# Activation biases as numbers, long runs for k, v and phi, and another order of the first loads

## The chip, the core and the metric

The kernel runs on one core of a Trainium2 chip. The metric is the device time of one execution in microseconds, as the median of several runs. In the profile PE is TensorE (PEld its weight loads), ACT is ScalarE, DVE is VectorE, POOL is GpSimd and SP is SyncE, which issues every DMA of this kernel.

## The reference

A memory attention (8 batches, 8 heads, 576 tokens, head size 64, 32 memory slots) followed by a feed-forward block with its own activation:

```python
a = softmax of phi over the tokens                  # b h s m
k_m = np.einsum('bhsm,bhsd->bhmd', a, k)
v_m = np.einsum('bhsm,bhsd->bhmd', a, v)
attn = softmax over m of (q @ k_m^T / sqrt(64))
x = (attn @ v_m) as 4608 tokens x 512
h = x @ w_in                                        # 512 x 2048, float64
sp = np.maximum(h, 0.0) + np.log1p(np.exp(-np.abs(h)))
out = ((h * erf(sp)) @ w_out)                       # 2048 x 512, float64
```

## The kernel before

The host lays the inputs out anew and hands the two weight matrices over as 64-bit integers. The chip turns these doubles into floats: `decode_1` clamps the high words on DVE (L142) and converts low and high words on ACT (L145, L146), `decode_2` joins them on DVE (L159, L162), and `decode_3` splits a w_out piece into a high and a low part (ACT L174 and L179, PE L177 and L178). A whole piece of weights has 1 MB and stands in a slot of the tag `wo`; smaller ones of half a MB stand in the three `raw` slots, which k and v use too.

A batch goes through `phi_max`, `phi_exp`, `kmvm` (k_m and v_m on PE, L275), `block_diag`, and `vw`, which multiplies v_m with w_in, so that the first matrix product of the feed-forward block takes the attention weights directly. The tokens of a batch are two units of 288. A unit has eight steps, one for each 256 columns of w_in: `ffn1` (PE L390, then tt = Tanh on ACT L397 and a product on DVE L398), three `factor`s (f on ACT L411 or L413, a product on DVE L414), `g_split` (ACT L422, DVE L423), and, up to three steps later, `ffn2` (PE L437), which sums into four PSUM tiles pso. After eight steps ACT L453 copies these out and SP stores them. The kernel has 128 steps.

The activation function is a product of the tt term and three factors with constants in a table. Each constant that is added ahead of the activation stands in a column of 128 x 1 in SBUF (`tb`, `fb`) and is given to the instruction as its bias:

```python
tb = column(GB, "tb")                                          # L104
nc.scalar.activation(tt[:, j], ps, AF.Tanh, bias=tb, scale=0.5)   # L397
```

k, v and phi are loaded so that chunk c of a tile holds tokens 128c to 128c + 127, one token to a partition, and the last chunk the remaining 64 tokens in 64 partitions. So a k/v tile of two heads comes in four DMAs (L210 and L214, for k and for v) with runs of 512 bytes, and phi in two (L193, L197) with runs of 1 KB.

The program is a list of tasks, written out ahead in the order of the steps, with the decoding and the next batch's tasks merged in. Loads have a queue of their own: each waits for a slot of its tag, and `FIRST` says in which order the first slots are given out. The final order on each engine is set by the framework's scheduler; on SP and on each engine instructions then issue in order. Batch 0's k/v tiles 0 and 1 must be there for the first `kmvm`, all four for the second, and w_in piece 0 for the first `vw`.

Of the kernel before, what the change touches and what calls it, by code (L numbers as in the profile page):

```python
# [8 lines left out]
F32 = mybir.dt.float32  # L9
# [4 lines left out]
AF = mybir.ActivationFunctionType  # L14
# [13 lines left out]
GC, GB = 0.27160413, -0.45239282  # L28
FACTORS = (
    ("Q", -1.75972316, 0.52065829),  # L30
    ("T", 0.56841178, 1.0199725, 0.42607248),
    ("T", 1.35008185, -1.89147316, 1.73987114),
)
# [3 lines left out]
def tile_memory_attention_then_erf_softplus_ffn(  # L37
    ctx: ExitStack,
    tc: tile.TileContext,
    qT: bass.AP,  # L40
    k: bass.AP,
    v: bass.AP,
    phi: bass.AP,
    phiT: bass.AP,
    w_in: bass.AP,
# [3 lines left out]
    nc = tc.nc  # L49
    P = 128  # L50
    B, _, S = qT.shape
    H = k.shape[2]
    D = 64
    M = 32
    DFF = w_in.shape[2]
# [1 line left out]
    NDM = DM // P  # L57
    NP_ = H // 2
    NG = 2
# [6 lines left out]
    SC = [(c * P, min(P, S - c * P)) for c in range((S + P - 1) // P)]  # L66
    RAW_BUFS = 3
    STAGED = 6
    FIRST = "wo phiT start phi wo raw raw wo raw start wo q".split()
    LEAD = 7  # L70
    WINDOW = {mybir.EngineType.DVE: (12, 28)}
    PO = 5
# [5 lines left out]
    const = ctx.enter_context(tc.tile_pool(name="const", bufs=1))  # L78
# [17 lines left out]
    ones = const.tile([P, P], F32, name="ones")  # L96
    nc.vector.memset(ones, 1.0)

    def column(value, name):
        t = const.tile([P, 1], F32, name=name)  # L100
        nc.vector.memset(t, value)
        return t

    tb = column(GB, "tb")  # L104
    fb = [column(f[1] if f[0] == "Q" else f[2], f"fb{i}") for i, f in enumerate(FACTORS)]
    fd = [f[2] if f[0] == "Q" else f[3] for f in FACTORS]

    w_in_sb = {}
    wo = {}
# [8 lines left out]
    st = {}  # L118
# [62 lines left out]
    def load_phiT(b, g):  # L181
# [4 lines left out]
        nc.sync.dma_start(out=t, in_=phiT[b, g * P : (g + 1) * P, :])  # L186
        st["phiT", b, g] = t

    def load_phi(b):
        t = att.tile([P, len(SC), H * M], F32, name="phi")  # L190
        n = S // P
        s0, ln = SC[-1]
        nc.sync.dma_start(  # L193
            out=t[:, :n], in_=phi[b, : n * P].rearrange("(c p) e -> p c e", p=P)
        )
        if ln < P:
            nc.sync.dma_start(out=t[:ln, n], in_=phi[b, s0 : s0 + ln])  # L197
        st["a", b] = t

    def load_kv(b, p):  # L200
        if b == 0 and p == NP_ - 1:
            t = wop.tile([P, len(SC), 2, 2, D], F32, name="kv", tag="wo")
        else:
            t = raw_pool.tile([P, len(SC), 2, 2, D], F32, name="raw")
        n = S // P
        s0, ln = SC[-1]
        h = 2 * p
        for x, src in enumerate((k, v)):
            src = src[b, :, h : h + 2]
            nc.sync.dma_start(  # L210
                out=t[:, :n, x], in_=src[: n * P].rearrange("(c p) h e -> p c h e", p=P)
            )
            if ln < P:
                nc.sync.dma_start(out=t[:ln, n, x], in_=src[s0 : s0 + ln])  # L214
        for j in range(2):
            st["kv", b, h + j] = t[:, :, :, j, :]

    def load_q(u):
        b, hf = divmod(u, 2)
# [19 lines left out]
    def phi_exp(b):  # L239
        ps = ps_a.tile([P, H * M], F32, name="psa")  # L240
        for g in range(NG):
            nc.tensor.matmul(
                out=ps[:, g * P : (g + 1) * P],
                lhsT=ones,
                rhs=st["diag", b][:, g],
                start=True,
                stop=True,
            )
        a = st["a", b]
        n = S // P  # L250
        ln = SC[-1][1]
        nc.vector.tensor_tensor(
            out=a[:, :n], in0=a[:, :n],
            in1=ps.unsqueeze(1).to_broadcast([P, n, H * M]), op=ALU.add,
        )
        if ln < P:
            nc.vector.tensor_tensor(out=a[:ln, n], in0=a[:ln, n], in1=ps[:ln], op=ALU.add)
            nc.scalar.activation(a[:ln, n], a[:ln, n], AF.Exp)
        nc.scalar.activation(a[:, :n], a[:, :n], AF.Exp)  # L259
        for g in range(NG):  # L260
            sm = st.pop(("psm", b, g))
            rs = small.tile([P, 1], F32, name=f"prs{g}")
            nc.vector.tensor_scalar_add(out=sm, in0=sm, scalar1=1e-9)
            nc.vector.reciprocal(out=rs, in_=sm)
            st["prs", b, g] = rs
# [108 lines left out]
    def products(w, x):  # L374
        return [(w[a], x[b]) for a, b in ((0, 0), (0, 1), (1, 0))]

    def ffn1(i, j):
        u, c = divmod(i, NPR)
        at, w = st["at", u], st["vw", u // 2, c]
        if j == 0:  # L380
            st["el", i] = (
                el.tile([P, 2, U], F32, name="tt"),
                el.tile([P, 2, U], F32, name="acc", bufs=3),
            )
        tt, acc = st["el", i]
        ps = ps_h.tile([P, U], F32, name="psh")
        parts = products(w, at)
        for k, (x, y) in enumerate(parts):
            for g in range(NG):
                nc.tensor.matmul(  # L390
                    out=ps,
                    lhsT=x[:, g, j * P : (j + 1) * P],
                    rhs=y[:, g, :],
                    start=(k + g == 0),
                    stop=(k == len(parts) - 1 and g == NG - 1),
                )
        nc.scalar.activation(tt[:, j], ps, AF.Tanh, bias=tb, scale=0.5)  # L397
        nc.vector.scalar_tensor_tensor(  # L398
            out=acc[:, j], in0=tt[:, j], scalar=1.0, in1=ps, op0=ALU.add, op1=ALU.mult
        )  # L400
        if j == 1 and u % 2 == 1:
            st.pop(("vw", u // 2, c))
        if j == 1 and c == NPR - 1:
            st.pop(("at", u))
# [72 lines left out]
    for c in range(NPR):  # L477
        n = NP_ if c < STAGED else 2
# [3 lines left out]
    def decode_steps(a, b):  # L482
        out = []
        for n in range(a, b):
            out.append((decode_1, *pieces[n]))
            for back, f in ((1, decode_2), (2, decode_3)):
                if n >= back:
                    out.append((f, *pieces[n - back]))
        if b == len(pieces):
            out += [(decode_2, *pieces[-1])] + [(decode_3, *p) for p in pieces[-2:]]  # L490
        return out
# [20 lines left out]
    for i in range(NPR):  # L512
        n = min(2 * i + 2 + LEAD, len(pieces))
# [5 lines left out]
    d = decode_steps(0, LEAD)  # L519
# [6 lines left out]
    for i in range(NS + 3):  # L526
        head = [(ffn1, i, 0)] if i < NS else []
        rest = []
        if 1 <= i <= NS:
            head += [(factor, i - 1, 1)]  # L530
        if i < NS:
            head += [(ffn1, i, 1)]
        if 1 <= i <= NS:
            rest += [(factor, i - 1, 2)]
        if i < NS:
            rest += [(factor, i, 0)]
        if 2 <= i <= NS + 1:
            rest += [(g_split, i - 2)]
        if i >= 3:
            rest = merge([(ffn2, i - 3, d) for d in range(NDM)], rest)  # L540
        prog += head + (merge(rest, side[i]) if i < NS else rest)

    def loads(f, a):
        if f is kmvm:
            kv = [("raw", load_kv, a[0], 2 * a[1] + r) for r in range(2)]
            if a == [0, NG - 1]:
                kv[1] = ("start", *kv[1][1:])
            return kv
        if f is decode_1:
            return [("wo" if a[3] == NP_ else "raw", load_weight, *a)]  # L550
        if f is phi_max:
            return [("start" if a == [0, 1] else "phiT", load_phiT, *a)]
        if f is phi_exp:
            return [("phi", load_phi, *a)]
        if f is scores:
            return [("q", load_q, a[0])]
        return []
# [28 lines left out]
    held, room = room, dict.fromkeys(room, 0)  # L586
    for tag in FIRST:
        room[tag] += 1
# [9 lines left out]
    for n, (f, *a) in enumerate(prog):  # L598
        start = len(traced)
        f(*a)  # L600
        for x in traced[start:]:
            if x.engine in issued:
                q, w = issued[x.engine], WINDOW[x.engine][n >= HEAD]
# [40 lines left out]
```

## Time and profile before

| | |
|---|---|
| median of 3 runs | 791.09 us (790.6 to 791.68) |
| the profiled execution | 790.4 us |
| its span, first to last instruction | 788.5 us |
| mean granted TensorE clock | 0.985 |
| DMA, whole span | 64.99 MB, 69514 packets, 82 GB/s |

The page gives the share of busy time of each engine over the whole span; the kernel has a beginning of about 100 us, in which the weights are decoded, and a long even part. A table by stretches of time and the chain of waits tell them apart. In the groups of instructions the number behind the busy time is the mean duration in ns; in the table of DMA issues the last number is the median time from issue to landing.

### The profile page before, as it was taken

How to read it: one execution, taken by the hardware profiler on the slowest of the kernel's cores; microseconds unless marked ns; L12 is line 12 of the kernel's file. 1: busy time of each engine (PE TensorE's matmuls, PEld its weight loads, DVE VectorE, ACT ScalarE, POOL GpSimd, SP SyncE). 2: the span in 40 equal slices, each digit the busy share in tenths (PEclk: the TensorE clock that was granted, in tenths of full speed). 3: DMA queues.
4: the chain of work that ended last, by engine and by line, in shares of the span. 5: the costliest groups of instructions: out<-in, count | busy, mean ns of one | idle time of the engine just before them, and what ended most of it. 6: DMA issues, size and time to landing. Idle time of an engine off the chain costs nothing.

```text
span 788.5 us, 15764 instructions
## 1 busy us (share of the span) xinstructions
PE 750.3 (95%) x6192; PEld 666.4 (85%) x6192; DVE 663.6 (84%) x1145; ACT 632.7 (80%) x1164; POOL 0.7 (0%) x6
## 2 busy tenths in 40 slices
PE   2668899999999999999999999999999999999998
PEld 1246678789988899888988899889988899889998
DVE  4699787889979897988979798989979897889874
ACT  4699778678887878878887878878888888788784
POOL 0000000000000000000000000000000000000000
PEclk9986999999999999999999999999999999999999
DMA  9983326303060203302060203302060201100000
GB/s 275 359 316 107 86 87 171 100 1 91 13 200 1 75 18 106 106 1 91 19 193 2 76 17 109 104 1 91 18 194 1 77 1 54 40 1 31 2 31 31
DMA packets 69514, 64.99 MB, mean 82 GB/s; under 512 B 4160, under 2 KB 62016, under 8 KB 68672
## 3 DMA queue, kind: packets, MB, share of 16 engines
q1 hardware_dynamic: 69440, 63.98, 26.2%
q8 instruction: 49, 0.80, 0.4%
q14 instruction: 25, 0.20, 0.1%
HBM read 54.53 MB, written 9.44 MB: 81 GB/s over the span
## 4 chain that ended last, share of the span: by engine, by line
PE 85%; ACT 7%; DMA 5%; DVE 2%; SPq 1%; issue 1%; ACTq 0%; DVEq 0%
PE pso L437 49%; PE psh L390 25%; PE psa L308 6%; PE psa L275 3%; DMA phiT<-phiT 1%; DMA w_in<-w_in 1%; DMA raw<-k 1%; PE psa L177 1%; DMA raw<-v 1%; DVE acc L414 1%; ACT f L413 1%; ACT tt L397 1%; ACT wo L179 1%; ACT w_in L145 1%; ACT w_out L146 1%
## 5 line engine op out<-in xcount | busy, mean ns | idle before, releaser
L437 PE MATMUL pso<-g_hi,wo 128*128 128x288 f32 x2048 | 436.3, 298 | 1.0 <-ACT g_hi L422 1.0
L437 PEld LDWEIGHTS pso<-g_hi,wo 128*128 128x128 f32 x2048 | 336.7, 189 | 26.5 <-issue 13.6
L414 DVE SCALAR_TENSOR_TENSOR acc<-f,acc 128x576 f32<-128x576 f32 x384 | 289.7, 754 | 34.7 <-ACT f L411 10.6
L437 PE MATMUL pso<-g_lo,wo 128*128 128x288 f32 x1024 | 302.3, 296 | 1.0 <-DVE g_lo L423 1.0
L437 PEld LDWEIGHTS pso<-g_lo,wo 128*128 128x128 f32 x1024 | 193.7, 189 | 2.6 <-DVE g_lo L423 1.3
L413 ACT ACTIVATE f<-tt,fb 128x576 f32<-128x576 f32 x256 | 185.1, 766 | 1.9 <-DVE acc L414 1.9
L397 ACT ACTIVATE tt<-psh,tb 128x288 f32<-128x288 f32 x256 | 121.9, 497 | 44.3 <-PE psh L390 43.0
L398 DVE SCALAR_TENSOR_TENSOR acc<-tt,psh 128x288 f32<-128x288 f32 x256 | 111.1, 449 | 23.6 <-ACT tt L397 22.9
L423 DVE SCALAR_TENSOR_TENSOR g_lo<-acc,g_hi 128x576 fp32r<-128x576 f32 x128 | 96.2, 751 | 28.7 <-ACT g_hi L422 25.9
L390 PE MATMUL psh<-at_hi,vw_hi 128*128 128x288 f32 x512 | 116.2, 308 | 4.3 <-ACT at_hi L115 2.6
L422 ACT ACTIVATE g_hi<-acc 128x576 fp32r<-128x576 f32 x128 | 87.3, 682 | 39.8 <-DVE acc L414 33.7
L390 PE MATMUL psh<-at_lo,vw_hi 128*128 128x288 f32 x512 | 110.9, 298 | 0.0
L390 PE MATMUL psh<-at_hi,vw_lo 128*128 128x288 f32 x512 | 109.8, 296 | 0.0
L390 PEld LDWEIGHTS psh<-at_hi,vw_hi 128*128 128x128 f32 x512 | 82.5, 191 | 23.3 <-DVE acc L414 10.1
L411 ACT ACTIVATE f<-tt,fb 128x576 f32<-128x576 f32 x128 | 99.5, 778 | 3.1
L390 PEld LDWEIGHTS psh<-at_hi,vw_lo 128*128 128x128 f32 x512 | 83.4, 190 | 2.8 <-issue 2.4
L390 PEld LDWEIGHTS psh<-at_lo,vw_hi 128*128 128x128 f32 x512 | 83.3, 191 | 0.9 <-issue 0.8
L308 PE MATMUL psa<-w_in,vm 64*32 64x512 f32 (+1 forms) x576 | 42.6, 561 | 6.1 <-ACT wo L179 4.7
L116 DVE TENSOR_TENSOR vw_lo<-psa,vw_hi 128x512 fp32r<-128x512 f32 (+1 forms) x72 | 43.0, 624 | 1.1 <-ACT vw_hi L115 0.9
L115 ACT ACTIVATE vw_hi<-psa 128x512 fp32r<-128x512 f32 (+1 forms) x72 | 36.2, 547 | 5.8 <-PE psa L308 5.7
L453 ACT ACTIVATE ot<-pso 128x288 f32<-128x288 f32 x60 | 23.2, 402 | 12.2 <-DMA outT<-ot 11.8
L275 PE MATMUL psa<-raw,phi 128*32 128x128 f32 x620 | 28.8, 291 | 3.5 <-ACT phi L259 2.4
(73 smaller groups left out, 437.6 us busy)
## 6 DMA issues: line engine op xcount, KB each, us to landing
q<-qT SPq DMA_DIRECT2D x16, 576.0 KB, 4.2
outT<-ot SPq DMA_DIRECT2D x60, 144.0 KB, 2.5
raw<-k SPq DMA_DIRECT2D x31, 256.0 KB, 3.4
raw<-v SPq DMA_DIRECT2D x31, 256.0 KB, 3.7
w_in<-w_in SPq DMA_DIRECT2D x6, 1024.0 KB, 8.7
w_out<-w_out SPq DMA_DIRECT2D x6, 1024.0 KB, 10.2
phiT<-phiT SPq DMA_DIRECT2D x16, 288.0 KB, 4.2
phi<-phi SPq DMA_DIRECT2D x8, 512.0 KB, 5.3
```

Of the source, the lines that this page charges most:

```text
L116: nc.vector.tensor_tensor(out=lo, in0=src, in1=hi.bitcast(F32), op=ALU.subtract)
L275: nc.tensor.matmul(out=ps[M * j : M * (j + 1), 0, :], lhsT=a[:ln, c, (4 * g + j) * M : (4 * g + j + 1) * M], rhs=kvt[j][:ln, c], start=(c ...
L308: nc.tensor.matmul(out=ps[par][p * M : (p + 1) * M, :], lhsT=w[rows, p, :], rhs=x[rows, p, :], start=True, stop=True,)
L390: nc.tensor.matmul(out=ps, lhsT=x[:, g, j * P : (j + 1) * P], rhs=y[:, g, :], start=(k + g == 0), stop=(k == len(parts) - 1 and g == NG - 1),)
L397: nc.scalar.activation(tt[:, j], ps, AF.Tanh, bias=tb, scale=0.5)
L398: nc.vector.scalar_tensor_tensor(out=acc[:, j], in0=tt[:, j], scalar=1.0, in1=ps, op0=ALU.add, op1=ALU.mult)
L411: nc.scalar.activation(f, tt, AF.Square, bias=fb[n])
L413: nc.scalar.activation(f, tt, AF.Tanh, bias=fb[n], scale=FACTORS[n][1])
L414: nc.vector.scalar_tensor_tensor(out=acc, in0=f, scalar=fd[n], in1=acc, op0=ALU.add, op1=ALU.mult)
L422: nc.scalar.activation(hi, acc, AF.Identity, scale=GC)
L423: nc.vector.scalar_tensor_tensor(out=lo, in0=acc, scalar=GC, in1=hi.bitcast(F32), op0=ALU.mult, op1=ALU.subtract)
L437: nc.tensor.matmul(out=o, lhsT=x[:, d * P : (d + 1) * P], rhs=y[:, j, :], start=(c + j + k == 0), stop=(c == NPR - 1 and j == 1 and k == l ...
```

## The change

The columns go; the constants are given to the instructions as numbers. k and v become one array `kv`, in which a token's two heads of k and v lie together. `load_tokens` gives partition p of the first 64 the tokens 5p to 5p + 4, and the other 64 partitions four tokens each: runs of 5 KB and 4 KB, in two DMAs of 64 partitions a tile, for phi too. Which token stands in which chunk differs, but alike for phi and kv, and `kmvm` sums over all of them. `FIRST` gives out the slots in another order: batch 0's data ahead of most weights.

```diff
-    FIRST = "wo phiT start phi wo raw raw wo raw start wo q".split()
+    FIRST = "phiT start phi raw raw wo raw start q wo wo wo wo".split()
-    def column(value, name):
-        t = const.tile([P, 1], F32, name=name)
-        nc.vector.memset(t, value)
-        return t
-
-    tb = column(GB, "tb")
-    fb = [column(f[1] if f[0] == "Q" else f[2], f"fb{i}") for i, f in enumerate(FACTORS)]
+    fb = [f[1] if f[0] == "Q" else f[2] for f in FACTORS]
+    def load_tokens(t, src):
+        n = S // P
+        ln = SC[-1][1]
+        m = len(SC)
+        if ln < P:
+            nc.sync.dma_start(
+                out=t[:ln], in_=src[: ln * m].rearrange("(p c) e -> p c e", c=m)
+            )
+            nc.sync.dma_start(
+                out=t[ln:, :n], in_=src[ln * m :].rearrange("(p c) e -> p c e", c=n)
+            )
+        else:
+            nc.sync.dma_start(out=t, in_=src.rearrange("(p c) e -> p c e", c=m))
     def load_phi(b):
         t = att.tile([P, len(SC), H * M], F32, name="phi")
-        nc.sync.dma_start(
-            out=t[:, :n], in_=phi[b, : n * P].rearrange("(c p) e -> p c e", p=P)
-        )
-        if ln < P:
-            nc.sync.dma_start(out=t[:ln, n], in_=phi[b, s0 : s0 + ln])
+        load_tokens(t, phi[b])
     def load_kv(b, p):
-        for x, src in enumerate((k, v)):
-            src = src[b, :, h : h + 2]
-            nc.sync.dma_start(
-                out=t[:, :n, x], in_=src[: n * P].rearrange("(c p) h e -> p c h e", p=P)
-            )
-            if ln < P:
-                nc.sync.dma_start(out=t[:ln, n, x], in_=src[s0 : s0 + ln])
+        load_tokens(t.rearrange("p c x h d -> p c (x h d)"), kv[b, p])
-        nc.scalar.activation(tt[:, j], ps, AF.Tanh, bias=tb, scale=0.5)
+        nc.scalar.activation(tt[:, j], ps, AF.Tanh, bias=GB, scale=0.5)
-        "k": k.transpose(0, 2, 1, 3),
-        "v": v.transpose(0, 2, 1, 3),
+        "kv": np.stack([k, v])
+        .reshape(2, B, H // 2, 2, S, D)
+        .transpose(1, 2, 4, 0, 3, 5)
+        .reshape(B, H // 2, S, 4 * D),
```

SP's queue from its first DMA on, before (a row gives line, tile written, array read and shape; the numbers tell tiles apart, raw and kv are k/v tiles of batch 0):

```order
L127 DMA w_in_115<-w_in 128x4x256
L186 DMA phiT_117<-phiT 128x576
L186 DMA phiT_119<-phiT 128x576
L193 DMA phi_121<-phi 128x4x256
L197 DMA phi_121<-phi 64x256
L132 DMA w_out_124<-w_out 128x1024
L210 DMA raw_126<-k 128x4x128
L214 DMA raw_126<-k 64x128
L210 DMA raw_126<-v 128x4x128
L214 DMA raw_126<-v 64x128
```

The remaining k/v tiles follow, with the second w_in piece (w_in_136) between them, then w_out_148, q_150 and the third w_in piece, w_in_152, as the 26th DMA. After, from the second k/v tile to the third w_in piece (ahead of these rows stand phiT twice, phi and the first k/v tile, two DMAs each for the latter two):

```order
L189 DMA raw_117<-kv 64x1280
L192 DMA raw_117<-kv 64x1024
L121 DMA w_in_120<-w_in 128x4x256
L189 DMA raw_122<-kv 64x1280
L192 DMA raw_122<-kv 64x1024
L189 DMA kv_125<-kv 64x1280
L192 DMA kv_125<-kv 64x1024
L215 DMA q_128<-qT 128x4x288
L126 DMA w_out_130<-w_out 128x1024
L121 DMA w_in_132<-w_in 128x4x256
L126 DMA w_out_134<-w_out 128x1024
L121 DMA w_in_136<-w_in 128x4x256
```

The first two w_out pieces and the first two w_in pieces moved behind batch 0's data, all or in part; the third w_in piece has the same transfers ahead of it, in 18 DMAs with itself counted.

ACT's queue at the first step's activations, before (tt and f are the activations, w_in_318 is the fifth whole w_in piece):

```order
L397 ACTIVATE tt_365<-psh_367,tb_103 128x288
L397 ACTIVATE tt_365<-psh_376,tb_103 128x288
L411 ACTIVATE f_385<-tt_365,fb0_105 128x576
L413 ACTIVATE f_435<-tt_365,fb1_107 128x576
L413 ACTIVATE f_447<-tt_365,fb2_109 128x576
L145 ACTIVATE w_in_318<-w_in_318 128x1024
```

And after (w_in_302 is that piece):

```order
L391 ACTIVATE tt_349<-psh_351 128x288
L139 ACTIVATE w_in_302<-w_in_302 128x1024
L391 ACTIVATE tt_349<-psh_360 128x288
L140 ACTIVATE w_in_302<-w_in_302 128x1024
L405 ACTIVATE f_369<-tt_349 128x576
L407 ACTIVATE f_419<-tt_349 128x576
L407 ACTIVATE f_431<-tt_349 128x576
```

The columns tb and fb are gone from the operands, and the fifth whole piece's decoding moved from behind the three f in between the two tt. In SP's queue this piece (29th DMA after) stands behind phi and q of the second batch and second unit.

More of the change, by code (lines that the diff above doesn't have):

```diff
@@ L40, in tile_memory_attention_then_erf_softplus_ffn @@
     qT: bass.AP,
-    k: bass.AP,
-    v: bass.AP,
+    kv: bass.AP,
     phi: bass.AP,
@@ L51, in tile_memory_attention_then_erf_softplus_ffn @@
     B, _, S = qT.shape
-    H = k.shape[2]
+    H = 2 * kv.shape[1]
     D = 64
@@ L187, in load_phiT @@
         st["phiT", b, g] = t
+    def load_tokens(t, src):
[11 more added lines that the diff above has]
+            nc.sync.dma_start(out=t, in_=src.rearrange("(p c) e -> p c e", c=m))
     def load_phi(b):
         t = att.tile([P, len(SC), H * M], F32, name="phi")
-        n = S // P
-        s0, ln = SC[-1]
-        nc.sync.dma_start(
-            out=t[:, :n], in_=phi[b, : n * P].rearrange("(c p) e -> p c e", p=P)
-        )
-        if ln < P:
-            nc.sync.dma_start(out=t[:ln, n], in_=phi[b, s0 : s0 + ln])
+        load_tokens(t, phi[b])
         st["a", b] = t
@@ L204, in load_kv @@
             t = raw_pool.tile([P, len(SC), 2, 2, D], F32, name="raw")
-        n = S // P
-        s0, ln = SC[-1]
-        h = 2 * p
-        for x, src in enumerate((k, v)):
-            src = src[b, :, h : h + 2]
-            nc.sync.dma_start(
-                out=t[:, :n, x], in_=src[: n * P].rearrange("(c p) h e -> p c h e", p=P)
-            )
-            if ln < P:
-                nc.sync.dma_start(out=t[:ln, n, x], in_=src[s0 : s0 + ln])
+        load_tokens(t.rearrange("p c x h d -> p c (x h d)"), kv[b, p])
         for j in range(2):
-            st["kv", b, h + j] = t[:, :, :, j, :]
+            st["kv", b, 2 * p + j] = t[:, :, :, j, :]
     def load_q(u):
```

## The prediction

> **What bounds the kernel now.** I began with the page: which engine is full, and what the chain that ended last is made of.
>
> ```profile
> span 788.5 us, 15764 instructions
> PE 750.3 (95%) x6192; PEld 666.4 (85%) x6192; DVE 663.6 (84%) x1145; ACT 632.7 (80%) x1164; POOL 0.7 (0%) x6
> PE 85%; ACT 7%; DMA 5%; DVE 2%; SPq 1%; issue 1%; ACTq 0%; DVEq 0%
> ```
>
> TensorE is near full over the whole span, but 13% of the chain is not TensorE. The table of stretches of time says where (busy us of each engine, granted clock, DMA share, GB/s):
>
> ```profile
> core 0: us, PE busy (x) PEld busy (x) DVE busy (x) ACT busy (x) POOL busy (x), PEclk, DMA share, GB/s
> 0.00:10.00 10.00, 0.00 (x0) 0.00 (x0) 1.94 (x8) 3.50 (x4) 0.70 (x6) 1.00 0.79 262
> 10.00:20.00 10.00, 4.52 (x44) 2.88 (x44) 7.80 (x14) 6.07 (x11) 0.00 (x0) 1.00 1.02 290
> 20.00:34.00 14.00, 8.79 (x67) 3.98 (x63) 6.89 (x8) 7.83 (x18) 0.00 (x0) 1.00 1.01 342
> 34.00:50.00 16.00, 10.51 (x54) 4.96 (x54) 15.86 (x23) 15.97 (x23) 0.00 (x0) 0.85 1.04 398
> 50.00:76.00 26.00, 20.36 (x105) 14.79 (x104) 25.05 (x38) 25.82 (x42) 0.00 (x0) 0.76 0.41 146
> 76.00:100.00 24.00, 21.79 (x139) 15.39 (x137) 20.05 (x40) 17.92 (x34) 0.00 (x0) 0.86 0.32 98
> 100.00:200.00 100.00, 100.00 (x819) 85.84 (x818) 85.12 (x159) 80.89 (x159) 0.00 (x0) 1.00 0.30 86
> 400.00:500.00 100.00, 99.38 (x851) 90.51 (x850) 85.86 (x150) 81.71 (x157) 0.00 (x0) 1.00 0.30 87
> 700.00:785.00 85.00, 85.00 (x669) 82.34 (x667) 67.66 (x109) 64.72 (x111) 0.00 (x0) 1.00 0.05 17
> ```
>
> From 100 us on TensorE is busy without a gap worth naming; ScalarE and VectorE have slack there, and the DMA engines work at 5 to 30%. Whatever the change does after 100 us is therefore hidden. The first 100 us are three regimes: the DMA engines are full up to 34 us while ScalarE and VectorE idle about half the time; then both of those are full to about 76 us; then TensorE takes over. The chain in order of time (start, length, what) gives the borders:
>
> ```profile
> 5.26 9.43 DMA raw<-k
> 16.54 7.48 DMA raw<-v
> 24.04 9.54 DMA w_in<-w_in
> 33.60 1.18 ACT w_in L145
> 37.09 1.01 ACT wo L174
> 38.11 1.05 ACT w_out L145
> 40.12 1.06 ACT w_out L146
> 50.85 0.78 ACT tt L397 x2
> 62.51 1.33 ACT f L413 x2
> 71.82 0.78 ACT tt L397 x2
> 73.49 1.33 PE pso L437 x4
> 92.31 0.79 ACT tt L397 x2
> 93.90 1.33 ACT f L413 x2
> 96.60 2.29 PE psh L390 x8
> ```
>
> So: loads until the third w_in piece lands and ScalarE takes it at 33.60; ScalarE alone to 73.49; TensorE to 91.7; ScalarE once more to 96.60; TensorE to the end. A microsecond gained counts if it moves 33.60, or shortens ScalarE's two stretches.
>
> **The biases.** Each of 640 ACTIVATEs loses its column operand. The price is read from instructions of the same shape with and without one (mean ns behind the busy time):
>
> ```profile
> L413 ACT ACTIVATE f<-tt,fb 128x576 f32<-128x576 f32 x256 | 185.1, 766 | 1.9 <-DVE acc L414 1.9
> L422 ACT ACTIVATE g_hi<-acc 128x576 fp32r<-128x576 f32 x128 | 87.3, 682 | 39.8 <-DVE acc L414 33.7
> L397 ACT ACTIVATE tt<-psh,tb 128x288 f32<-128x288 f32 x256 | 121.9, 497 | 44.3 <-PE psh L390 43.0
> L453 ACT ACTIVATE ot<-pso 128x288 f32<-128x288 f32 x60 | 23.2, 402 | 12.2 <-DMA outT<-ot 11.8
> ```
>
> That is 766 - 682 = 84 ns for f and 497 - 402 = 95 ns for tt: 384 x 0.084 + 256 x 0.095 = 57 us of ScalarE in all. Nearly all of it lies under a full TensorE and is worth nothing; without that cover ScalarE would still have VectorE, the busier of the two after 100 us (85 against 81), behind it. On the chain lie the ones between 33.60 and 73.49 (three pairs of tt, two triples of f: 6 x 0.095 + 6 x 0.084 = 1.07 us) and those between 91.7 and 96.6 (one pair, one triple: 0.44 us). In the first stretch VectorE is next: 15.86 + 25.05 = 40.91 busy of 42 us, so 1.1 us is all it could give, and it would be full afterwards. I take half there and all of the second: 1.0 us, bounds 0 and 1.5. The four removed MEMSETs are in the idle first microseconds: nothing.
>
> **The loads.** The sizes, from the table of DMA issues (KB each, us to landing):
>
> ```profile
> q<-qT SPq DMA_DIRECT2D x16, 576.0 KB, 4.2
> raw<-k SPq DMA_DIRECT2D x31, 256.0 KB, 3.4
> w_in<-w_in SPq DMA_DIRECT2D x6, 1024.0 KB, 8.7
> phiT<-phiT SPq DMA_DIRECT2D x16, 288.0 KB, 4.2
> phi<-phi SPq DMA_DIRECT2D x8, 512.0 KB, 5.3
> raw<-k SPq DMA_DIRECT2D x31, 32.0 KB, 3.1
> phi<-phi SPq DMA_DIRECT2D x8, 64.0 KB, 5.0
> ```
>
> The third w_in piece has the same things ahead of it in SP's queue before and after: phiT 2 x 288, phi 576, four k/v tiles of 576, q 576, and w_in, w_out, w_in, w_out, w_in of 1024: 9152 KB, 9.37 MB. Only the order inside and the form of phi and k/v (2880 KB, 2.95 MB) differ. Let the first 10 us move 2.62 MB again (262 GB/s, the start included); the other 6.75 MB at the 398 GB/s of 34:50, where weights move in long runs, take 17.0 us, so the piece lands at 27.0 if phi and k/v run at that rate too. This is the low end. No row shows long runs into 64 partitions. The high end is half of 398, as if half the partitions took half the bandwidth: 2.95 MB then need 14.8 us in place of 7.4, landing at 34.4. Between them I take the row in which k and v move now, 290 GB/s (runs a tenth as long, 512 bytes by the code, but nearly all in 128 partitions): 10.2 us, landing at 29.8. It is the same data, and the two differences pull in opposite directions.
>
> ScalarE takes the piece about 0.5 us later: the w_out piece before it lands 2.6 us earlier (1.05 MB at 398), and behind that landing come three ACTIVATEs of 1.05, 1.01 and 1.06 us. So 33.60 becomes 27.5, **30.3** or 34.9: -6.1, **-3.3** or +1.3 us. VectorE has 7 us idle in 20:34 to follow. The set of ScalarE's instructions ahead of the piece stays the same; only where it waits changes.
>
> One new wait stands behind it. The fifth whole w_in piece is now asked for between the two tt of the first step (last order fence above), four activations sooner in ScalarE's queue, and the second batch's phi and q are ahead of it in SP's queue: 7072 KB after the third piece, 7.24 MB, 18.2 us at 398, and 0.5 us more with phi at 290. It lands at 29.8 + 18.7 = 48.5; ScalarE gets there at 51.2 - 3.3 = 47.9. That gives back 0.6 us, and all of ScalarE's queue waits behind it, the second tt first.
>
> The loads of batches 1 to 7 come in two DMAs a tile in place of four. Even at half rate a tile (0.59 MB) takes 3.0 us against 2.0, while three raw tiles are held ahead and TensorE stays full: nothing, unless a wait on raw shows up at kmvm.
>
> **Sum.** -3.3 - 1.0 + 0.6 = -3.7 us: a span of 784.8 for 788.5. The profiled execution took 790.4 us (1.9 around its span), 0.7 under the median of 791.09; against the median this is **787.4 us**.
>
> **Rivals.** Long runs at full rate: the two halves of a tile overlap in the queue. For it: the DMA share is 1.02 at only 290 GB/s in 10:20 and 1.04 at 398 in 34:50, so the short runs cost a quarter of the rate now. Against it: the two DMAs of a tile never cover 128 partitions at once. -6.1 - 1.0, no new wait (45.2 against 45.1): **784.0**.
>
> Half rate: the piece is taken at 34.9 (+1.3), and the fifth w_in piece lands at 34.4 + 18.2 + 1.5 = 54.1, where ScalarE stands at 51.2 + 1.3 = 52.5, a wait of 1.6. With 1.0 back from the biases this is +1.9, **793.0**: slower. The place is phi, k and v of batch 0 in SP's queue ahead of the weights; the first term changes sign where they take 13.5 us, at about 218 GB/s. For it: nothing has measured the opposite. Against it: now, too, each tile ends in a 64-partition DMA and lands in 3.1 to 5.0 us. The Trainium skill's page "SBUF — State Buffer", section "Door 1: The DMA port swizzle", says that partitions 0 to 63 reach only 8 of 16 ports, and gives 196 GB/s for them at 1 MiB. By that figure, an estimate, 2.95 MB need 15.1 us and the whole would come to about 793.3. No run here shows it yet; it is the case of this paragraph, and its chance is below.
>
> No head start: ScalarE comes 3 us earlier and then waits for VectorE, which keeps all its work (40.91 of 42 us busy) and sets the end of the second regime. For it: VectorE is as full as ScalarE. Against it: its 7 us of idle time in 20:34 go with the earlier weights. It leaves the 0.44 us of biases: **790.6**.
>
> **Chances.** My forecast (785.4 to 789.4) 0.40; full rate 0.25; half rate 0.20; no head start 0.15. About 0.2% (1.6 us) is what a measurement of this kernel can tell from no change. Faster by more: 0.37 of the forecast, 0.25, and 0.02 of the last: 0.64. Slower by more: 0.13 of half rate (0.07 of it fall within) and 0.02: 0.15. Within: 0.03 + 0.07 + 0.11 = 0.21. The range of 8 in 10 takes in both rates: 782.5 to 793.0.
>
> **What would show it.** f near 682 and tt near 402 ns; the third w_in piece taken by ScalarE near 30 us; GB/s in 4 to 20 us near 290 (full: 380 and more; half: near 200); the first tt at 47 to 48 in place of 50.85; TensorE without gaps from about 93 in place of 96.6. The forecast fails beyond its range if TensorE's clock does otherwise. It stood at
>
> ```profile
> 70.00:80.00 10.00, 7.80 (x40) 5.68 (x41) 10.00 (x17) 8.68 (x15) 0.00 (x0) 0.66 0.19 52
> ```
>
> that is, 3.4 us of full-speed time lost there, part of it in TensorE's own stretch of the chain (73.49 to 91.7). One such loss more or less as TensorE starts, or a gap of several us after 100 us, would be as large as the whole effect.

## The result, and the profile after

The changed kernel takes 797.45 us (median, 795.37 to 798.56) where the kernel before, in runs on the same chip, takes 790.85: a ratio of 1.0084, 95% interval 1.0055 to 1.0114. It is slower by 6.6 us; 787.4 was predicted. The profiled execution took 798.06 us with a span of 796.3.

The page of the kernel after:

```profile
span 796.3 us, 15678 instructions
PE 752.0 (94%) x6192; PEld 664.4 (83%) x6192; DVE 663.7 (83%) x1141; ACT 576.7 (72%) x1164; POOL 0.7 (0%) x6
PE 85%; DMA 5%; ACT 5%; DVE 4%; issue 0%; SPq 0%; DVEq 0%; ACTq 0%
```

ScalarE has lost 56 us of work (632.7 before), as worked out, and the kernel is longer all the same. The groups of instructions give the new durations, and two waits that have grown or are new (the last one in batch 0 alone):

```profile
L407 ACT ACTIVATE f<-tt 128x576 f32<-128x576 f32 x256 | 161.8, 673 | 0.7 <-DVE acc L408 0.7
L391 ACT ACTIVATE tt<-psh 128x288 f32<-128x288 f32 x256 | 98.8, 407 | 48.4 <-PE psh L384 47.3
L447 ACT ACTIVATE ot<-pso 128x288 f32<-128x288 f32 x60 | 22.7, 402 | 20.7 <-DMA outT<-ot 20.0
L269 PE MATMUL psa<-raw,phi 128*32 128x128 f32 x620 | 29.2, 291 | 4.9 <-DMA raw<-kv 4.9
```

The same stretches of time as before:

```profile
0.00:10.00 10.00, 1.59 (x4) 1.01 (x4) 3.68 (x11) 3.80 (x8) 0.70 (x6) 1.00 0.79 205
10.00:20.00 10.00, 3.14 (x40) 1.92 (x41) 1.30 (x3) 3.82 (x6) 0.00 (x0) 1.00 1.03 250
20.00:34.00 14.00, 8.68 (x62) 3.79 (x63) 7.78 (x11) 7.84 (x17) 0.00 (x0) 1.00 1.04 378
34.00:50.00 16.00, 9.20 (x28) 3.31 (x26) 16.00 (x21) 15.58 (x20) 0.00 (x0) 0.96 1.03 344
50.00:76.00 26.00, 18.88 (x107) 12.98 (x108) 24.96 (x38) 24.82 (x42) 0.00 (x0) 0.76 0.52 192
100.00:200.00 100.00, 97.69 (x834) 86.38 (x835) 89.17 (x167) 77.87 (x164) 0.00 (x0) 1.00 0.37 100
400.00:500.00 100.00, 99.55 (x862) 89.65 (x859) 84.12 (x146) 73.26 (x159) 0.00 (x0) 1.00 0.30 79
700.00:785.00 85.00, 85.00 (x676) 81.36 (x675) 69.85 (x116) 59.20 (x115) 0.00 (x0) 1.00 0.05 15
```

Two things are to be seen. With the DMA engines as busy as before (shares of 0.79 and 1.03), the first 20 us move 205 and 250 GB/s in place of 262 and 290. And from 200 us on TensorE is as full as before, at the same clock, so this table alone does not tell where most of the time went.

What tells it is a mark that every batch sets on TensorE: the four small matmuls of `phi_exp`, once a batch. In order of time (start, length, what), those of batches 1, 2 and 7, before:

```profile
119.41 0.61 PE L242 MATMUL psa<-diag,ones 128*128 128x128 f32 x4
207.38 0.60 PE L242 MATMUL psa<-diag,ones 128*128 128x128 f32 x4
648.79 0.60 PE L242 MATMUL psa<-diag,ones 128*128 128x128 f32 x4
```

and after:

```profile
123.09 0.61 PE L236 MATMUL psa<-diag,ones 128*128 128x128 f32 x4
207.79 0.61 PE L236 MATMUL psa<-diag,ones 128*128 128x128 f32 x4
656.21 0.60 PE L236 MATMUL psa<-diag,ones 128*128 128x128 f32 x4
```

So the beginning loses 3.7 us, the next batch gives 3.3 back, and the five batches to the last mark lose 7.0 (448.4 for 441.4; 0.4 more come behind it), in the part of which the prediction said that nothing could count there. The marks of one kernel can stand a few ffn matmuls earlier or later in TensorE's stream than those of another, so a difference of 1 us in them is not read as an effect.

What TensorE does differently is seen in its own rows. `vw_pair` is a group of eight matmuls on 64 x 32 pieces of the array, each with two records (entries of the trace). Before, a whole group, with the first ffn2 matmul behind it:

```profile
274.22 0.29 PE L437 MATMUL pso<-g_hi,wo 128*128 128x288 f32 x1
274.44 1.09 PE L308 MATMUL psa<-w_in,vm 64*32 64x512 f32 x16
275.46 0.40 PE L437 MATMUL pso<-g_hi,wo 128*128 128x288 f32 x1
```

After, the same group:

```profile
275.21 1.05 PE L302 MATMUL psa<-w_in,vm 64*32 64x512 f32 x6
276.20 0.40 PE L431 MATMUL pso<-g_hi,wo 128*128 128x288 f32 x1
...
276.96 0.29 PE L431 MATMUL pso<-g_hi,wo 128*128 128x288 f32 x1
277.19 1.07 PE L302 MATMUL psa<-w_in,vm 64*32 64x512 f32 x10
278.19 0.40 PE L431 MATMUL pso<-g_hi,wo 128*128 128x288 f32 x1
```

Six records and ten take 1.0 us each, and sixteen take 1.0 us too. From the group's start to the ffn2 matmul behind it pass 2.98 us, in which six ffn2 matmuls are done as well, 0.80 us at the pace that they have by themselves (0.79 for the six from 273.43 to 274.22 in the kernel before): 2.18 for 1.02, so the break costs 1.16 us. TensorE shows as busy throughout. In TensorE's stream of the kernel after, one group is broken in each of batches 2 to 6, and none in the kernel before; that has one group of batch 1 in three pieces, which the kernel after has whole:

```profile
149.49 1.06 PE L308 MATMUL psa<-w_in,vm 64*32 64x512 f32 x8
151.46 1.06 PE L308 MATMUL psa<-w_in,vm 64*32 64x512 f32 x6
153.44 1.04 PE L308 MATMUL psa<-w_in,vm 64*32 64x512 f32 x2
```

### The profile page after: what moved, and what is told of

Read it like the earlier page. It is cut to its first block, busy times and chain, and to the rows that moved or that the text cites. A ratio compares the mean times of both kernels' runs of the same rounds, so it can differ in the third digit from the quotient of the medians.

```text
span 796.3 us, 15678 instructions
## 1 busy us (share of the span) xinstructions
PE 752.0 (94%) x6192; PEld 664.4 (83%) x6192; DVE 663.7 (83%) x1141; ACT 576.7 (72%) x1164; POOL 0.7 (0%) x6
## 4 chain that ended last, share of the span: by engine, by line
PE 85%; DMA 5%; ACT 5%; DVE 4%; issue 0%; SPq 0%; DVEq 0%; ACTq 0%
PE pso L431 49%; PE psh L384 25%; PE psa L302 6%; PE psa L269 3%; DMA outT<-ot 2%; DMA kv<-kv 2%; DMA raw<-kv 1%; PE psa L171 1%; ACT f L407 1%; DVE w_out L156 1%; DVE w_out L153 1%; ACT wo L168 1%; PE psa L285 0%; ACT f L405 0%; DMA raw<-w_out 0%
## 5 line engine op out<-in xcount | busy, mean ns | idle before, releaser
L431 PEld LDWEIGHTS pso<-g_hi,wo 128*128 128x128 f32 x2048 | 335.5, 188 | 28.1 <-issue 12.2
L407 ACT ACTIVATE f<-tt 128x576 f32<-128x576 f32 x256 | 161.8, 673 | 0.7 <-DVE acc L408 0.7
L391 ACT ACTIVATE tt<-psh 128x288 f32<-128x288 f32 x256 | 98.8, 407 | 48.4 <-PE psh L384 47.3
L392 DVE SCALAR_TENSOR_TENSOR acc<-tt,psh 128x288 f32<-128x288 f32 x256 | 110.1, 447 | 28.3 <-ACT tt L391 27.5
L405 ACT ACTIVATE f<-tt 128x576 f32<-128x576 f32 x128 | 87.8, 686 | 3.2
L302 PE MATMUL psa<-w_in,vm 64*32 64x512 f32 (+1 forms) x576 | 44.5, 561 | 5.7 <-ACT wo L173 4.6
```

The lines of the kernel that those rows point to most:

```text
L302: nc.tensor.matmul(out=ps[par][p * M : (p + 1) * M, :], lhsT=w[rows, p, :], rhs=x[rows, p, :], start=True, stop=True,)
L391: nc.scalar.activation(tt[:, j], ps, AF.Tanh, bias=GB, scale=0.5)
L392: nc.vector.scalar_tensor_tensor(out=acc[:, j], in0=tt[:, j], scalar=1.0, in1=ps, op0=ALU.add, op1=ALU.mult)
L405: nc.scalar.activation(f, tt, AF.Square, bias=fb[n])
L407: nc.scalar.activation(f, tt, AF.Tanh, bias=fb[n], scale=FACTORS[n][1])
L431: nc.tensor.matmul(out=o, lhsT=x[:, d * P : (d + 1) * P], rhs=y[:, j, :], start=(c + j + k == 0), stop=(c == NPR - 1 and j == 1 and k == l ...
```

## The experiments

Theory O: the even part is longer because the scheduler wrote TensorE's stream in another order. Rival L: because of the loads. Rival F: because of the new order of the first loads. Every ratio below is to the kernel before, run on the same chip.

**One part at a time.** The first three make one part of the change each, the fourth takes the numbers out of the kernel after. The edits are those of the diff above.

> The kernel before with numbers in place of the seven bias columns and nothing else; loads and their front order stay. Theory O (order): with cheaper ScalarE work the scheduler writes TensorE's stream in another order. In this kernel's stream one of the four vw_pair groups (eight 32x512 matmuls on w_in and vm) is broken into 3+5 or 2+6 with ffn matmuls between, in five of the seven later batches, where the kernel before has them whole. In the trace after, a broken group costs 0.98 + 1.00 us where a whole one costs 1.02, and each piece another 0.24 on the ffn matmul behind it: about 1.2 us each, 6 us in five. It gives 795 to 797 us, with a period of a batch near 89 to 90 us instead of 88. Theory L (loads): what the kernel after loses comes with its long-run loads through 64 partitions; numbers alone then give 789 to 791. Theory F (front order): the same 789 to 791.

> The kernel before with k, v and phi in long runs (two 64-partition transfers each), its old front order and its bias columns. TensorE's stream is that of the kernel before, row for row, with no broken vw_pair group. Theory O: nothing is added after 200 us; the loads can only move the first 125 us, so 789 to 793 us. Theory L: each later batch loses its 0.9 us to slow kv and phi loads and to output stores that wait behind them, as in the kernel after, and the result is 796 to 798.

> The kernel before with the new front order alone (batch 0's loads ahead of most weights), short runs and bias columns as before. Its TensorE stream has no broken vw_pair group at all; the kernel before has one in its second batch (pieces of 8, 6 and 2 matmul records at 149.5 to 154 us of its trace, 0.97 to 0.99 us each, so some 2.4 us more than a whole one). Theory O: 786 to 791 us: the 2.4 us come back, and late weights take up to 3 us at the head. Theory F: the front order itself costs what the first tt shows in the kernel after, 3.9 us, and it is kept to the end: 794 to 796.

```diff
-        nc.scalar.activation(tt[:, j], ps, AF.Tanh, bias=GB, scale=0.5)     # e4, from the kernel after
+        nc.scalar.activation(tt[:, j], ps, AF.Tanh, bias=tb, scale=0.5)     # and fb likewise
```

> The kernel after with bias columns again: long runs and new front order stay, and only the numbers go. TensorE's stream has no broken vw_pair group in batches 2 to 7 (one piece of 1 split off in the second batch). Theory O: the 6 us of five broken groups go, 790 to 793 us, although ScalarE is 56 us busier. Theory L and theory F: it stays at 797 to 799, since loads and front order are those of the kernel after.

| | median us | ratio (95%) | batch 1's mark | batch 2's mark to batch 7's |
|---|---|---|---|---|
| before | 790.76 | 1 | 119.4 | 441.4 |
| e1 numbers only | 796.71 | 1.0076 (1.0054 to 1.0097) | 120.2 | 446.6 |
| e2 loads only | 798.73 | 1.0102 (1.0075 to 1.0129) | 127.1 | 443.0 |
| e3 front order only | 792.98 | 1.0040 (1.0026 to 1.0055) | 121.8 | 441.6 |
| e4 loads and front order | 791.21 | 1.0012 (0.9998 to 1.0025) | 118.7 | 441.6 |

Numbers alone lengthen the even part by 5.2 us, and without them it has its old length within 0.2 us in e3 and e4 and within 1.6 in e2: theory O holds for the even part, and L and F fall there as its main cause. Why cheaper biases change the order was not tried; e1 differs from the kernel before in nothing else. But e2 lost 8 us where theory O allowed 2 at most. That is near the number of theory L, but not in its place: 7.7 us are lost before batch 1's mark:

```profile
127.14 0.61 PE L242 MATMUL psa<-diag,ones 128*128 128x128 f32 x4
215.39 0.61 PE L242 MATMUL psa<-diag,ones 128*128 128x128 f32 x4
658.41 0.61 PE L242 MATMUL psa<-diag,ones 128*128 128x128 f32 x4
```

So the loads are expensive after all, in the beginning, and with the new front order they are no worse than the short runs (e4 against e3). e3 falls between its two expectations: the group of batch 1 is whole, but little of its 2.4 us shows at batch 2's mark (209.0), and the beginning is 2.4 us longer.

**Groups kept whole, and long runs in all partitions.** In e5 order dependencies keep a group together; e6 repeats e2 with another spread of the tokens.

```diff
+            if x.engine == mybir.EngineType.PE:                      # e5, in the loop over prog
+                if f in (vw_pair,) and n >= HEAD:
+                    for y in stream[-24:] if group[0] is not f else stream[-1:]:
+                        tc.add_manual_dep(x, y.name, near, reason="whole group")
+                    group[:] = [f, x, 24]
+                elif group[2] > 0:
+                    tc.add_manual_dep(x, group[1].name, near, reason="whole group")
+                    group[:] = [None, group[1], group[2] - 1]
+                stream.append(x)
```

> The kernel after with one thing added: in the even part, order dependencies keep each vw_pair group of eight matmuls together on TensorE (the group's first matmul is ordered behind the 24 TensorE matmuls written ahead of it, the next 24 behind its last). Numbers, long runs and front order stay, and the stream has no broken vw_pair group. Theory O: the break itself is the cost, 5 groups by about 1.2 us: 790.5 to 792.5 us. Rival W (wait): a group is broken because its second half would have to wait for PSUM or for the split on ScalarE and VectorE; kept whole, TensorE stands in that wait instead, and the time stays at 796 to 798.

```diff
+        nc.sync.dma_start(                                            # e6, load_tokens
+            out=t[:, :n], in_=src[: n * P].rearrange("(p c) e -> p c e", c=n)
+        )
+        if ln < P:
+            nc.sync.dma_start(out=t[:ln, n], in_=src[n * P :])
```

> As in e2 the kernel before with its old front order and bias columns, and k, v and phi in long runs; but the runs go to all 128 partitions (tokens 4p to 4p+3 to partition p, 4096 bytes), and only the last 64 tokens, 1024 bytes each, go to 64 partitions. Theory P (partitions): e2's 8 us are the half rate of 64-partition transfers and what it does to the weights queued beside them (8192-byte packets of whole weights then take 480 to 500 ns in place of 309). With 128 partitions 10 to 34 us runs at 290 GB/s and more as in the kernel before or better: 785 to 792 us. Rival Q (queue): long runs cost by themselves, because a transfer of few large packets holds the queue longer ahead of the one that is waited for: 796 to 800 as in e2.

e5: 794.36 us, ratio 1.0039 (1.0024 to 1.0055); batch 2's mark to batch 7's 443.5, that is 4.9 of the 7.0 us back; rival W falls, though the median stays 3.4 us above the kernel before and lies between the two expectations. e6: 789.00 us, 0.9972 (0.9962 to 0.9983): 9.7 us less than e2, with long runs in other partitions (4 KB, and 1 KB for the last 64 tokens). The DMA rate in slices of 1 us from the start shows it, first in e2:

```profile
GB/s 0 0 141 264 328 370 342 298 239 232 243 270 255 289 231 248 242 212 234 286 223 281 289 257 254 248 241 279 275 248 337 317 386 408 403 427 438 427 390 414
DMA packets 4058, 11.27 MB, mean 282 GB/s; under 512 B 318, under 2 KB 830, under 8 KB 3679
```

then in e6:

```profile
GB/s 0 0 133 299 332 361 321 393 371 342 439 393 397 342 307 328 369 426 408 350 346 343 378 380 374 406 403 407 464 416 412 391 412 457 418 387 401 397 428 418
DMA packets 5426, 14.35 MB, mean 359 GB/s; under 512 B 390, under 2 KB 1222, under 8 KB 4913
```

From 10 to 30 us e2 stays between 212 and 289 although whole weights are queued between the kv tiles, and e6 between 307 and 464. The kernel before moved 12.74 MB in these 40 us. So long runs do help, by about 13%, if they fill all partitions. In halves they are slow, and they slow the weights that are in flight with them. The traces' packets from 10 to 30 us tell the two apart (median durations): those of 8192 bytes, which weights have, take 506 ns in e2 and 309 in e6 and in the kernel before; those of 4096 bytes, nearly all of k and v, take 282 ns in halves and 168 through all partitions. In the kernel after, where batch 0's data go ahead of the weights, the slow time is shorter:

```profile
GB/s 0 37 265 355 153 289 236 237 235 248 220 181 215 358 389 225 227 231 226 223 183 265 457 396 401 377 391 412 426 428 371 383 390 414 463 391 360 389 389 393
DMA packets 4536, 12.23 MB, mean 306 GB/s; under 512 B 341, under 2 KB 853, under 8 KB 4152
```

181 to 248 GB/s from 6 to 13 us and 183 to 231 from 15 to 21, with the halves running by themselves, and near 400 from 22 us on.

**More groups whole.** The dependencies of e5 around scores and kmvm as well; e8 has the loads of e6 besides.

```diff
-                if f in (vw_pair,) and n >= HEAD:
+                if f in (vw_pair, scores, kmvm) and n >= HEAD:
```

> The kernel after with the same order dependencies around three kinds of groups: vw_pair, scores and kmvm. In every kernel so far the second scores group of a batch is broken into 4+12 records (0.61 + 0.63 us where a whole one takes 0.65, and 0.24 on the ffn matmul behind the extra piece: 0.8 us), and one kmvm group into 4+36 (0.34 more and 0.24: 0.6 us). Theory O: besides the 6 us of vw_pair, 6 to 7 batches give 0.8 + 0.6 us each, some 8 to 9 us: 781 to 785 us. Rival W: kmvm and scores wait for loads and for VectorE, TensorE stands there, and the time is 788 to 792.

> e7 with the loads of e6: numbers, new front order, long runs through 128 partitions, and the three kinds of groups whole. Theory P with O: batch 0's kv lands some 4 us earlier than in the kernel after (22.3 us), weights follow earlier, and the head is 1 to 4 us shorter than in e7: 778 to 783 us. If the head is bound by VectorE's decoding (busy 16.00 of 16 us from 34 to 50 us in the kernel after), earlier loads give nothing: as e7 within 1 us.

e7 took 831.16 us (1.0507, 1.0483 to 1.0531), e8 802.21 (1.0144, 1.0121 to 1.0166): both far off. The waits of TensorE in e7 (us in total, times, longest):

```profile
PE pso L431 <- ACT ot L447: 30.2, 7, 5.4
```

In e8, with the faster loads, the same wait is 15.9 us. We read it so: nothing may pass a group of kmvm or scores that waits for its data, so ffn2 and the copies of pso into ot come late. No run tries this by itself. A group is worth keeping whole where TensorE doesn't wait for its inputs (vw_pair in e5), not everywhere.

**The break by itself.** e9 breaks groups of the kernel before: `vw_pair` for c = 2 becomes two tasks of four matmuls, and dependencies keep the ffn matmuls between them.

```diff
-                tasks[2 * NPR - VL + c + 1] += [(vw_pair, b, c)]
+                tasks[2 * NPR - VL + c + 1] += [(vw_half, b, c, 0), (vw_half, b, c, 1)]   # c == 2
```

> The kernel before, columns, short runs and old front order kept, with one vw_pair group of each later batch broken on purpose into 4+4 matmuls with ffn matmuls between; the rest of TensorE's stream is the same row for row. Six batches get one break more and the second batch two, eight in all. Theory O: 8 by 1.2 us (a second piece of 1.0 us less what the whole group loses, and 0.24 on the ffn matmul behind it): 799 to 801 us. Rival W (a break only marks a wait and costs little by itself): 790 to 793.

> e1 (numbers alone) with the vw_pair groups of the even part kept whole as in e5. Theory O: e1's 796.7 less five breaks of 1.2 us and less the three pieces of the second batch (2.4 us): 788.5 to 791. By what e5 gave back against the kernel after, 3.1 us: 793 to 794, and something else in the order that the numbers bring costs the rest. Rival W: 796 to 798.

e9: 799.90 us, 1.0117 (1.0095 to 1.0138), 8.8 us for eight breaks. e10, e1 with the dependencies of e5: 788.87 us, 0.9971 (0.9955 to 0.9988), batch 2's mark to batch 7's 441.8. So e1's loss was the order. That e10 is 2.2 us faster than the kernel before isn't shown to be the numbers: that kernel has two breaks in batch 1, some 2.3 us, and columns with whole groups were not tried. The groups of `vw_pair` matmuls from 150 to 780 us (busy us behind the bar) in the kernel before, the kernel after and e10:

```profile
L308 PE MATMUL psa<-w_in,vm 64*32 64x512 f32 x448 | 32.6, 601 | 0.0
```

```profile
L302 PE MATMUL psa<-w_in,vm 64*32 64x512 f32 x448 | 35.7, 601 | 0.0
```

```profile
L302 PE MATMUL psa<-w_in,vm 64*32 64x512 f32 x448 | 30.5, 601 | 0.0
```

The count and the mean of 601 ns are the same; the busy time grows by 1.04 us with every piece more (28 in e10, 30 before, 33 after).

**Full-rate loads with the rest.** No new edits, only combinations.

> Bias columns, the loads of e6 (long runs through 128 partitions) and the new front order. The front order alone cost 2.2 us with short runs (e3), and took 7.5 us less with the half-rate loads than the old order did (e4 against e2). If the front order only pays by keeping half-rate transfers apart from the weights, it gives nothing to full-rate loads: 789 to 792 us, no better than e6's 789.0. If batch 0's early data are worth something once they come at full rate: 785 to 788.

> e6 (long runs through 128 partitions, old front order) with numbers, and the vw_pair groups kept whole. Theory O: numbers cost nothing but the broken groups, and ScalarE's 56 us less are hidden beside TensorE except some 1 us at the head: 787 to 789 us. If the numbers' order costs more than the breaks, as e5 hints: 791 to 793.

> e5 (numbers, new front order, whole vw_pair groups) with the long runs sent to 128 partitions in place of two halves. Theory P: the 3 us that e5 still loses come from the half-rate loads (in e5 TensorE waits 1.5 us after 150 us for stores of ot, and its lag on e10 is 4 us at 180 us): 782 to 787 us. Rival F: front order and numbers together lose them in the head, whatever the loads: 790 to 794.

> e5 with the old short-run loads: numbers, new front order, whole vw_pair groups. Theory P: without half-rate loads it stands near e10 (788.9) plus what the front order costs with short runs (e3: 2.2 us): 788 to 791 us. Rival F: 793 to 796.

| | loads | front order | biases | median us | ratio (95%) |
|---|---|---|---|---|---|
| e6 | 128 partitions | old | columns | 789.00 | 0.9972 (0.9962 to 0.9983) |
| e11 | 128 partitions | new | columns | 784.98 | 0.9934 (0.9914 to 0.9954) |
| e12 | 128 partitions | old | numbers, whole groups | 784.51 | 0.9925 (0.9905 to 0.9946) |
| e13 | 128 partitions | new | numbers, whole groups | 788.53 | 0.9974 (0.9957 to 0.9991) |
| e5 | halves | new | numbers, whole groups | 794.36 | 1.0039 (1.0024 to 1.0055) |
| e14 | short runs | new | numbers, whole groups | 789.96 | 0.9987 (0.9970 to 1.0005) |

e5 against e13 and e14: the halves cost what e5 still lost, 4 to 6 us; e14 lies where theory P had it, e13 1.5 us above, and both below rival F. e11 is as fast as its second expectation had it at best, and e12 is 2.5 us faster than either of its two; both are some 6 us faster than the kernel before. The effects do not add: with columns the new front order gains 4 us (e11 against e6), with numbers it loses 4 (e13 against e12), and with columns and the new front order the halves cost nothing beside the short runs (e4 against e3) but 6 us beside 128 partitions (e4 against e11).

Where e13 loses is seen in its trace. It is 0.2 us behind e12 at batch 1's mark, 0.4 at batch 2's, 3.5 at batch 3's and 4.0 at batch 7's. Between batches 2 and 3 TensorE waits once for VectorE, and its clock falls for a moment:

```profile
281.13 0.53 PE L378 MATMUL psh<-at_hi,vw_hi 128*128 128x288 f32 x2 [1.87 <-DVE acc L386]
275.00:285.00 10.00, 8.13 (x52) 7.89 (x51) 9.19 (x20) 5.73 (x13) 0.00 (x0) 0.86 0.10 32
```

e12 has 9.78 of 10 us busy there, at a clock of 1.00. So 3.1 of the 4 us are lost between two marks after 200 us. At batch 1's mark the front order has given nothing with numbers, and 6 us with columns (114.95 in e11 for 120.98 in e6). Why, and whether e13's other executions have the same wait, stays open.

## Why the prediction was wrong

**"Whatever the change does after 100 us is therefore hidden"** is the step that failed, with 5 to 6 us of the 7.0 that the even part lost. The view was right, TensorE is full there before and after. But a full engine can be made longer by the order of its own work: five breaks of 1.16 us are 5.8 of the 7.0 us. Keeping the groups whole gave 4.9 back (e5), eight breaks more cost 8.8 (e9), and e10 took the loss of the numbers away. The change was read as one of durations and loads; that TensorE's stream has other groups in batches 2 to 6 could have been read off before any run.

**The loads term, -3.3 us,** failed too, in its rate and in its path. It took 290 GB/s for the halves; the kernel after has 181 to 248 while they run (fence above), and ScalarE takes the third w_in piece at 35.82 in place of 33.60, beyond the high end of 34.9:

```profile
35.82 1.23 ACT L139 ACTIVATE w_in<-w_in 128x1024 int32<-128x1024 uint32 x1
```

The row shows no wait: ScalarE comes to the piece straight from its own work, not from a landing. The path goes another way. With the weights behind batch 0's data, VectorE gets its first piece 9.4 us later, before and after:

```profile
8.09 0.69 DVE L142 TENSOR_SCALAR w_in<-w_in 128x1024 f32<-128x1024 f32 x1 [7.06 <-DMA w_in<-w_in]
17.51 0.69 DVE L136 TENSOR_SCALAR w_in<-w_in 128x1024 f32<-128x1024 f32 x1 [7.22 <-DMA w_in<-w_in]
```

By 34 us it has 12.8 us of work behind it in place of 16.6 (the tables by stretches), and it is all but full from there to 76. These 3.9 us are as many as the first tt is late by (54.59 for 50.68 by ScalarE's rows, where 47 to 48 was forecast); batch 1's mark is 3.7 late. The same holds for e4 (2.5 less work, first tt 2.5 late) and e11 (1.2 more, 1.2 early), whose VectorE is full from 34 us on too; e3, where it is not quite full, has 1.3 less and a first tt 0.1 early. So "only where it waits changes" was wrong: the weights land too late for the idle time in 20:34 that the prediction gave VectorE to follow in (6.2 of its 14 us stay idle), and its decoding stands behind 34 us instead. A better rate alone would not have given the forecast. With the same front order ScalarE takes the piece at 33.32 with short runs (e3), for which the term has 30.3, and at 30.72 through 128 partitions (e11), for which it has 27.5, both straight from its own work:

```profile
33.32 1.28 ACT L145 ACTIVATE w_in<-w_in 128x1024 int32<-128x1024 uint32 x1
30.72 1.20 ACT L145 ACTIVATE w_in<-w_in 128x1024 int32<-128x1024 uint32 x1
```

The rival of half rate had the slow halves and their place, and gave +1.9 for the whole beginning; it kept the same path, and it lacked that weights in flight with the halves slow down too (e2). That VectorE sets the end of the second regime is in the rival "No head start", but there VectorE starts no later than before. The two pulls that the prediction let cancel are not of one size: long runs through all partitions raise the rate (e6), halves cost about a third of it. The Trainium skill's page "SBUF — State Buffer", section "Door 1: The DMA port swizzle", lets partitions 0 to 63 reach half of the ports; e2 against e6 agrees, and with two halves queued one behind the other the rate is some 220 GB/s where the page has 196 for one transfer of 1 MiB. The page "DMA: Bandwidth & Descriptors" of the Trainium skill, section "Rules for kernel authors", advises one transfer through 128 partitions in place of two halves; e6 does so for all but the last 64 tokens of a tile, and is 9.7 us faster than e2.

**The biases term, -1.0 us,** had the right durations (673 and 407 ns where 682 and 402 were forecast). Its worth in time is not shown by itself: at batch 1's mark e1 is 0.8 us behind the kernel before and e10 1.8 ahead, and both have another order of the beginning.

**The new wait for the fifth whole w_in piece, +0.6 us,** did not come: ScalarE takes it at 54.89 straight behind the first tt. Everything ahead of it was later.

**The loads of later batches** were put at nothing "unless a wait on raw shows up at kmvm". The 4.9 us of that wait in the kernel after all lie in batch 0's `kmvm`. ScalarE's ot waits longer for its stores, 20.0 us for 11.8, but not for the slow loads alone: e1, with short runs, has 17.2, and e2, with the slow loads, 12.2. After 150 us TensorE waits 1.2 us for ot in the kernel after.

**No gap** of several us appeared after 100 us, and TensorE's clock did not decide: it was 0.76 from 50 to 76 us as before, 0.93 for 0.86 from 76 to 100, and 1.00 from there to 785. The list of what would make the prediction wrong lacked the case that came: more busy time for the same work. One reading was a little off: the part of the chain that is not TensorE is 15% by the page, not 13%; nothing hangs on it.

## What to carry to other kernels

Where an engine is full, compare its instruction stream before and after any edit, also one that only makes another engine's work cheaper: a scheduler may answer with another order, and small matmuls that share the array lose their company when a long one comes between them. Send long runs to all 128 partitions in one transfer; in halves they slow the transfers around them as well. Try the parts of a change one by one, since a loss in one can hide a gain in another.

## What the runs showed of the hardware

Sixteen records of 64 x 32 matmuls with 601 ns each are done in 1.02 us, and 10, 6 or 2 of them take 0.97 to 1.0: a broken group pays the full 1.0 us again, and 0.1 us at either edge. The Trainium skill's page "TensorE: Matmul & The Clock Gate", section "Part 3: Packing small matmuls — row/col tiling", says that matmuls in different tiles of the array run at the same time; these rows agree, and show what a break costs. All the while TensorE shows as busy. And transfers into half of the partitions slow whole ones in the same queue: weights and halves together move 255 GB/s (the mean of e2 from 10 to 30 us) against 384 in e6, and the weights' packets of 8192 bytes take 506 ns for 309.
